# Attention and rational MLP in one kernel: keys and queries transposed by VectorE from 32 by 32 blocks, first softmax in two equal parts

## The chip, the cores and the metric

One core of one Trainium2 chip runs the whole kernel. The metric is the device time of that core in microseconds (us). The engines are called as the profile calls them: PE is TensorE's matmul, PEld its weight load, DVE is VectorE, ACT is ScalarE, POOL is GpSimd, SP is SyncE, whose queue issues the kernel's DMAs.

## The reference

There are 8 batches of 8 heads, each with 576 tokens of 64 columns, and 32 "pack" rows `p` per head.

```python
def sm_attn(qq, kk, vv):
    s = scale * np.matmul(qq, kk.transpose(0, 1, 3, 2))
    s = s - np.max(s, axis=-1, keepdims=True)
    a = np.exp(s)
    a = a / (np.sum(a, axis=-1, keepdims=True) + 1e-09)
    return np.matmul(a, vv)
p_packed = sm_attn(p, k, v)
out = sm_attn(q, p_packed, p_packed)
...
h = x @ w_in                      # x: 4608 tokens of 512, w_in 512 x 2048
P = a[0] + a[1] * h + a[2] * h2 + a[3] * h3
Q = 1.0 + np.abs(b[0]) * np.abs(h) + np.abs(b[1]) * h2
g = P / (Q + 1e-06)
return (g @ w_out).astype(np.float32)
```

The weights of the MLP come as float64 and are converted on the chip.

## The kernel before

**A planner sets the order.** The kernel's operations are recorded by a `Planner` (line 32) and issued by its `issue` (line 212) in the order of a list schedule. A table of costs per engine, a rate for DMAs (`DMA_RATE`, line 48) and the edges between operations set their ranks. Every engine then runs its own list strictly in order, so a row that waits holds back all rows behind it on that engine. All compute instructions carry one line, L216, in the profile; they are told apart by the names of their tiles.

**The MLP.** The hidden layer is worked in units of half a batch (288 tokens) by 256 of the 2048 hidden columns; a batch has 16 units. A unit (`hidden`, line 681) multiplies with PE into two tiles `h`; ACT, DVE and POOL turn them into the rational function (tiles `Y`, `U`, `sq`, `V`, 288 or 576 columns wide), and split the result into `gh` and `gl`. Three units later PE multiplies these with `w_out` into `acc` (`acc_block`, line 758). The leftover 64 tokens of a batch are gathered over two batches in `G` and multiplied in `remainder` (line 730).

**The attention of the next batch** (`attention`, line 476) is a generator whose pieces are laid between the units of the batch before. The first batch's attention stands ahead of all units, and the second's falls into the stretch in which the weights are still converted. One batch's attention goes so:

1. Keys come in two tiles of four heads, `k0` and `k1` (`load`, line 428), into a ring `nat` of two buffers that keys, values and queries share. A tile holds the first 512 tokens, 4 successive tokens of a head per partition. The 64 leftover tokens of keys and queries go into a tile `rkq`, those of the values into `rv`.
2. `transposed` (line 497) turns a tile with 8 PE transposes of 128 by 128 into PSUM, in two PSUM banks, and ACT copies each bank (128x512) into the big tile `KX` (`kx` in the profile). Four more PE transposes and a copy bring the leftover keys (`krem`).
3. Scores of the pack rows against the keys; softmax in two parts, of 256 and 320 keys. Each part keeps its own maximum. Afterwards small DVE operations and an ACT exponential (lines 548 to 554) work out factors `F` that bring the parts together.
4. PE transposes the exponentials, multiplies them with the values (one product for each part), and DVE adds the parts with `tensor_scalar` and `scalar_tensor_tensor` (lines 598 to 603). When the product has read the values, the two query loads may start (lines 593 to 595).
5. Queries are transposed as the keys were, 16 PE transposes and 4 copies, plus 4 and 2 for the leftover tokens. The next batch's keys and leftovers are loaded as buffers come free.
6. Second scores, DVE's 32 by 32 transposes of them out of PSUM, softmax, DVE transposes back, and the split into `AH` and `AL`, which the next batch's units read.

`KX` exists once, so the next batch's keys can't be put there before this batch's `AH` and `AL` are done.

Of the kernel before, what the change touches and what calls it, by code (L numbers as in the profile page):

```python
# [18 lines left out]
AF = mybir.ActivationFunctionType  # L19
# [12 lines left out]
class Planner:  # L32
# [59 lines left out]
    def transfer(self, args):  # L92
        size = mybir.dt.size(args[1].dtype)
        run = 1
        for step, n in reversed(args[1].ap):
            if step != run:
                break
            run *= n
        n = 1
        for _, m in args[1].ap:  # L100
            n *= m
        return n * size / self.DMA_RATE[run * size >= 1024]

    def price(self, engine, calls):
        if engine != "tensor":
# [83 lines left out]
    def order(self):  # L189
        n = len(self.ops)  # L190
        self.costs = [self.price(*x) for x in self.ops]
        self.transfers = [self.transfer(calls[0][1]) if engine == "sync" else 0 for engine, calls in self.ops]
        before = self.edges()
        after = [[] for _ in range(n)]
        for i, x in enumerate(before):
            for j in x:
                after[j].append(i)
        sync = [x[0] == "sync" for x in self.ops]
        rank = list(range(n))
        best = None  # L200
# [7 lines left out]
        self.t0 = best[1]; self.deps = dict(enumerate(before))  # L208
        self.end = best[0]
        return sorted(range(n), key=lambda i: (best[1][i], i))  # L210

    def issue(self):
# [35 lines left out]
def attention_rational_ffn(  # L248
# [48 lines left out]

    full_ring = Ring(sb, "full", 1, [P, DM])
    neg = full_ring.next([P, P], F32R)
    nat_ring = Ring(sb, "nat", 2, [P, 4 * NS * D])  # L300
    pn_ring = Ring(sb, "pn", 1, [P, NG, 2, D])
    rkq_ring = Ring(sb, "rkq", 1, [P, H, D])

    rv_ring = Ring(sb, "rv", 1, [P, H // 2, D])

# [117 lines left out]

    NAT, AH, AL, PPT = {}, {}, {}, {}

    def load(bb, what):
        if bb >= B:
            return  # L430
        if what == "rem":

            r, rv, pn = NAT[bb, "r"], NAT[bb, "rv"], NAT[bb, "p"] = rkq_ring.next(), rv_ring.next(), pn_ring.next()
            nc.sync.dma_start(r[0:REM], k[bb, :, NS * P : T, :].rearrange("h p d -> p h d"))
# [4 lines left out]
            for i in range(2):  # L439
                src = q[bb, 4 * i : 4 * i + 4, NS * P : T, :].rearrange("h (p x) d -> p h (x d)", x=2)  # L440
                r2 = r[REM + HREM * i : REM + HREM * (i + 1)].rearrange("p (h x) d -> p h (x d)", x=2)
                nc.sync.dma_start(r2, src)
            for i in range(2):
                src = v[bb, 4 * i : 4 * i + 4, NS * P : T, :].rearrange("h p d -> p h d")
                nc.sync.dma_start(rv[REM * i : REM * (i + 1)], src)
            return
        x, g = what[0], int(what[1])
        src = {"k": k, "q": q, "v": v}[x][bb, 4 * g : 4 * g + 4, 0 : NS * P, :]
        if bb == 0 and x != "k":
            if g == 0:  # L450
                NAT[x] = w_ring.at(NCH - 2 + "vq".index(x), [P, 2, 4 * NS * D], F32)
            t = NAT[x][:, g, :]
        else:
            t = nat_ring.next()
# [21 lines left out]
    def attention(bb):  # L476
# [30 lines left out]
        for g in range(2):  # L507
# [1 line left out]
            if bb > 0:  # L509
                load(bb, f"v{g}")  # L510
            yield
        rkq = NAT[bb, "r"]
        t = bank(bb)
        for j in range(NJ):
            nc.tensor.transpose(t[:, j * P : (j + 1) * P], rkq[:, 2 * j : 2 * j + 2, :], ident)
        nc.scalar.copy(krem, t.rearrange("p (j c) -> p j c", j=NJ)[:, :, 0:REM])
        t = bank(bb)
        for r in range(NG):
            nc.tensor.transpose(t[:, r * P : (r + 1) * P], NAT[bb, "p"][:, r, :, :], ident)
        nc.scalar.copy(pT, t[:, 0 : NG * P].rearrange("p (r c) -> p r c", r=NG))  # L520
        yield


        KEYS = ((0, 2 * P), (2 * P, T))
        of = lambda a, r: a.rearrange("p (x r) -> p x r", r=NG)[:, :, r]
        for r in range(NG):
            t = [bank(bb)[:, 0 : c1 - c0] for c0, c1 in KEYS]
            tiles(
                (
                    (t[x][cols(j), 0 : 2 * P], pT[rows(i), r, cols(j)], kmain[rows(i), r, j, :]),  # L530
                    dict(start=True, stop=True),
                )
                for j in range(NJ)
                for x, i in ((0, 1 - r), (1, r))
            )
# [12 lines left out]
        nc.vector.tensor_tensor(nbm, nb[:, 0:2], nb[:, 2:4], ALU.min)  # L548
        nc.vector.tensor_sub(xr(f), two(nbm), xr(nb))
        nc.scalar.activation(f, f, AF.Exp)  # L550
        nc.vector.tensor_mul(fs, f, sm)
        nc.vector.scalar_tensor_tensor(tot, fs[:, 0:2], 1e-9, fs[:, 2:4], ALU.add, ALU.add)
        nc.vector.reciprocal(rec, tot)
        nc.vector.tensor_mul(xr(F), xr(f), two(rec))
        yield

        for r in range(NG):
            t = bank(bb)
            for s in range(NS):
                nc.tensor.transpose(t[:, s * P : (s + 1) * P], KX[:, r, s * P : (s + 1) * P], ident)  # L560
            nc.scalar.copy(KX[:, 2 + r, 0 : NS * P], t)
            if r == 1:

                t = bank(bb)
                for i in range(NG):
                    o = slice(i * P, (i + 1) * P)
                    nc.tensor.transpose(t[:, o], KX[:, i, T - P : T], ident)
                    nc.tensor.transpose(t[0:REM, o], KX[:, i, NS * P : T], ident)
                nc.scalar.copy(eTr, t[:, 0 : NG * P])
# [1 line left out]

        t = bank(bb)
        rv = NAT[bb, "rv"]
        for r in range(NG):
# [22 lines left out]
        twice = lambda o: o.rearrange("p (i d) -> p i d", i=1).broadcast_to([P, 2, D])  # L597
        for r in range(NG):
            o = pp[:, r]
            nc.vector.tensor_scalar(o, twice(t[:, 2 * r * D : (2 * r + 1) * D]), F[:, r : r + 1], None, ALU.mult)  # L600
            nc.vector.scalar_tensor_tensor(
                o, twice(t[:, (2 * r + 1) * D : (2 * r + 2) * D]), F[:, 2 + r : 3 + r], o, ALU.mult, ALU.add
            )
            nc.tensor.transpose(t[:, (2 + r) * P : (3 + r) * P], pT[:, r, :], ident)
        nc.scalar.copy(PPT[bb], t[:, 2 * P :].rearrange("p (r c) -> p r c", r=NG))
        yield
        for g in range(2):
            transposed("q", g)
            load(bb + 1, f"k{g}")
            if g == 0:  # L610
                t = bank(bb)
                for j in range(NJ):
                    nc.tensor.transpose(t[:, j * P : (j + 1) * P], rkq[:, 2 * j : 2 * j + 2, :], ident)
                src = t.rearrange("p (i r y a c) -> p r y a i c", r=NG, y=2, a=2, i=2)[:, :, 1]
                for r in range(NG):
                    nc.scalar.copy(qx[:, r, :, HMAIN:HALF].rearrange("p (a i) c -> p a i c", a=2), src[:, r])
                load(bb + 1, "rem")
            yield

# [138 lines left out]
    def acc_block(u, i):  # L758
# [10 lines left out]
        if i == 0:  # L769
            O[bb, x] = o_ring.next()  # L770
        o = O[bb, x]
        ov = out[bb * T : bb * T + NS * P, :].rearrange("(p i x) m -> p x i m", i=2, x=2)[:, x]
        if u == NU - 1 and i == 1:
            nc.vector.tensor_copy(o[:, i, :], acc)
        else:
# [94 lines left out]
```

## Time and profile before

| | |
|---|---|
| median of 3 runs | 822.48 us (822.13 to 823.46) |
| the profiled execution | 823.16 us |
| its span, first to last instruction | 821.4 us |
| mean granted TensorE clock | 0.969 |
| stretch from 204 to 763 us: clock, PE busy | 1.00, 555.6 of 559 us |
| the DMA queue's share of the 16 engines' time | 20.9% |

Until about 140 us the weights are loaded and converted, from about 160 us to 763 us the kernel is in a steady state, and the last 58 us hold the last units. In the fences below a row of the groups names the line, the engine, the operation, `out<-in`, the shapes and the count, then busy us and mean ns of one, then the idle time of the engine before it with what ended it. A row of a timeline or of the chain has the start, the length, the engine and what it ran. A row of the stretches names the stretch and its length, then busy us and instructions of each engine, the granted clock, the mean share of the DMA engines and GB/s.

### The profile page before, as it was taken

How to read it: one execution, taken by the hardware profiler on the slowest of the kernel's cores; microseconds unless marked ns; L12 is line 12 of the kernel's file. 1: busy time of each engine (PE TensorE's matmuls, PEld its weight loads, DVE VectorE, ACT ScalarE, POOL GpSimd, SP SyncE). 2: the span in 40 equal slices, each digit the busy share in tenths (PEclk: the TensorE clock that was granted, in tenths of full speed). 3: DMA queues.
4: the chain of work that ended last, by engine and by line, in shares of the span. 5: the costliest groups of instructions: out<-in, count | busy, mean ns of one | idle time of the engine just before them, and what ended most of it. 6: DMA issues, size and time to landing. Idle time of an engine off the chain costs nothing.

```text
span 821.4 us, 15529 instructions
## 1 busy us (share of the span) xinstructions
PE 774.1 (94%) x5584; PEld 613.7 (75%) x5584; DVE 693.6 (84%) x1296; ACT 691.5 (84%) x1566; POOL 460.9 (56%) x462
## 2 busy tenths in 40 slices
PE   5677788999999999999999999999999999999997
PEld 3355565888877877788877877788877878778886
DVE  2999999888898788988798778988798788998873
ACT  5898888899797879999888869999888889898872
POOL 0006455755487546755577445755578445856663
PEclk9678798999999999999999999999999999999999
DMA  8973241010400212010400203010400210000001
GB/s 250 387 253 105 104 123 27 26 57 26 123 27 1 81 50 87 27 52 31 123 26 1 81 20 117 27 52 30 123 27 1 77 37 31 26 1 27 26 2 39
DMA packets 50941, 56.06 MB, mean 68 GB/s; under 512 B 13488, under 2 KB 40112, under 8 KB 50864
## 3 DMA queue, kind: packets, MB, share of 16 engines
q1 hardware_dynamic: 50864, 55.07, 20.9%
q8 instruction: 44, 0.72, 0.4%
q14 instruction: 33, 0.27, 0.1%
HBM read 45.62 MB, written 9.44 MB: 67 GB/s over the span
## 4 chain that ended last, share of the span: by engine, by line
PE 75%; DVE 12%; ACT 7%; DMA 2%; issue 1%; SPq 1%; POOL 0%; DVEq 0%; ACTq 0%; POOLq 0%
PE acc L216 36%; PE h L216 23%; PE at L216 16%; DVE Y L216 5%; DVE small L216 3%; DMA m<-in_moe_w_in_dram 2%; DVE w L216 2%; ACT w L216 1%; ACT V L216 1%; ACT m L216 1%; DVE V L216 1%; ACT Y L216 1%; SPq L216 1%; ACT U L216 1%; ACT kx L216 1%
## 5 line engine op out<-in xcount | busy, mean ns | idle before, releaser
L216 PE MATMUL acc<-w,gh 128*128 128x512 f32 x1024 | 330.6, 401 | 4.4 <-ACT w L216 4.4
L216 PEld LDWEIGHTS acc<-w,gh 128*128 128x128 f32 x1024 | 186.6, 190 | 47.8 <-issue 5.8
L216 POOL TENSOR_TENSOR U<-U,sq 128x576 f32<-128x576 f32 x118 | 168.8, 1431 | 73.1 <-ACT U L216 31.6
L216 POOL TENSOR_TENSOR gl<-Y,gh 128x512 fp32r<-128x512 f32 x128 | 166.2, 1299 | 65.0 <-ACT gh L216 32.2
L216 PE MATMUL acc<-w,gl 128*128 128x512 f32 x512 | 198.4, 401 | 0.0
L216 PE MATMUL h<-AH,m 128*128 128x288 f32 x1024 | 193.6, 308 | 4.5 <-DVE Y L216 4.0
L216 PEld LDWEIGHTS h<-AH,m 128*128 128x128 f32 x1024 | 160.0, 192 | 36.2 <-DVE Y L216 16.9
L216 ACT ACTIVATE Y<-h,abS 128x288 f32<-128x288 f32 x256 | 128.2, 513 | 27.6 <-PE h L216 23.8
L216 DVE TENSOR_TENSOR Y<-Y,h 128x288 f32<-128x288 f32 x256 | 111.3, 447 | 40.0 <-ACT sq L216 20.0
L216 DVE SCALAR_TENSOR_TENSOR Y<-Y,abS,V 128x576 f32<-128x576 f32 x128 | 103.4, 808 | 39.3 <-ACT V L216 38.6
L216 DVE SCALAR_TENSOR_TENSOR Y<-Y,abS,h 128x288 f32<-128x288 f32 x256 | 126.4, 507 | 3.3
L216 ACT ACTIVATE sq<-h 128x288 f32<-128x288 f32 x236 | 98.3, 422 | 33.9 <-PE h L216 31.9
L216 PEld LDWEIGHTS acc<-w,gl 128*128 128x128 f32 x512 | 96.7, 190 | 28.4 <-issue 7.7
L216 PE MATMUL h<-AL,m 128*128 128x288 f32 x512 | 112.7, 300 | 0.0
L216 POOL COPY G<-Y 128x64 f32<-128x64 f32 x128 | 34.6, 270 | 135.9 <-DVE Y L216 102.9
L216 ACT ACTIVATE U<-h 128x288 f32<-128x288 f32 x256 | 100.9, 426 | 8.5 <-DVE V L216 6.6
L216 ACT ACTIVATE V<-U,one 128x576 f32<-128x576 f32 x128 | 99.0, 774 | 8.1 <-DVE Y L216 6.5
L216 DVE SCALAR_TENSOR_TENSOR Y<-V,Y 128x576 f32<-128x576 f32 x128 | 96.1, 751 | 2.0
L216 DVE SCALAR_TENSOR_TENSOR V<-U,V 128x576 f32<-128x576 f32 x128 | 96.2, 751 | 0.0
L216 ACT CAST gh<-Y 128x512 fp32r<-128x512 f32 x128 | 82.0, 641 | 5.2 <-DVE Y L216 3.5
L216 ACT ACTIVATE V<-V 128x576 f32<-128x576 f32 x128 | 85.4, 667 | 0.4
L216 PEld LDWEIGHTS h<-AL,m 128*128 128x128 f32 x512 | 84.1, 192 | 0.3
(123 smaller groups left out, 908.3 us busy)
## 6 DMA issues: line engine op xcount, KB each, us to landing
nat<-in_k_dram SPq DMA_DIRECT2D x16, 512.0 KB, 4.0
out_dram<-o SPq DMA_DIRECT2D x15, 512.0 KB, 3.1
w<-in_moe_w_out_dram SPq DMA_DIRECT2D x14, 512.0 KB, 4.4
nat<-in_v_dram SPq DMA_DIRECT2D x14, 512.0 KB, 3.9
nat<-in_q_dram SPq DMA_DIRECT2D x14, 512.0 KB, 5.0
m<-in_moe_w_in_dram SPq DMA_DIRECT2D x8, 512.0 KB, 9.5
w<-in_moe_w_in_dram SPq DMA_DIRECT2D x8, 512.0 KB, 11.0
rkq<-in_k_dram SPq DMA_DIRECT2D x8, 128.0 KB, 4.2
```

The costliest lines, as they stand in the source:

```text
L216: getattr(getattr(self.nc, engine), name)(*args, **kwargs)
```

## The change

Nothing changes for the first batch but the place of its `rkq` tile. For the other seven:

- **Loads.** A key or query tile now has all 576 tokens of four heads. It comes in four DMAs, for even and odd tokens (`i`) and for the two halves of 32 columns (`y`). Each writes 32 partitions: token `2 t + i` of a run of 64 lies in partition `64 i + 32 y + t`, as 36 pieces of 32 columns, 128 bytes each. Before, a tile was one DMA whose pieces were 1 KB. The tile `rkq` and its loads are gone. Values come in two DMAs per tile with pieces of 512 bytes, in another order of tokens. `rv` comes in four DMAs.
- **Transposes.** DVE transposes the 32 by 32 blocks, straight from the loaded tile into `KX`: two instructions of 128x576 per tile. PE's transposes of keys and queries and ACT's copies of them are gone, as are those of `rkq`.
- **First softmax.** Two equal parts of 288 keys with one common maximum (one `tensor_scalar` per row group takes the larger and scales it), so that the factors `F`, the extra exponential and the second half of the sum of parts fall away; the two products with the values become one. The matmuls of the scores are cut into 256 and 32 columns, since the second part begins in the middle of the tokens' order.
- **Planner and output.** `DMA_RATE` gets a third value, 100, for pieces under 256 bytes. Rows of the output go to other places in the same tile, in pieces of the same size.

```diff
-    DMA_RATE = 190.0, 370.0
+    DMA_RATE = 100.0, 190.0, 370.0
...
+            src = src.rearrange("h t d -> (h t) d")
+            for i in range(2):
+                for y in range(2):
+                    o = 64 * i + 32 * y
+                    blocks = src[:, 32 * y : 32 * y + 32].rearrange("(a t i) d -> i t a d", t=32, i=2)[i]
+                    nc.sync.dma_start(t[o : o + 32].rearrange("p (a d) -> p a d", d=32), blocks)
+            return
...
         def transposed(x, g):
-            for r in range(NG):
+            for r in range(NG if bb > 0 else 0):
+
+                src = NAT[bb, f"{x}{g}"].rearrange("p (j r c) -> p r j c", j=2, r=NG)[:, r]
+                nc.vector.transpose(qx[:, r, 2 * g : 2 * g + 2, :], src)
+            for r in range(NG if bb == 0 else 0):
                 t = bank(bb)
...
-        KEYS = ((0, 2 * P), (2 * P, T))
+        KEYS = ((0, 2 * P), (2 * P, T)) if bb == 0 else ((0, HALF), (HALF, T))
...
+                for x in range(2):
+                    nc.vector.reduce_max(mx[:, 2 * x + r : 2 * x + r + 1], t[x], axis=AX.X)
+                bias = nbm[:, r : r + 1]
+                nc.vector.tensor_scalar(bias, mx[:, r : r + 1], mx[:, 2 + r : 3 + r], -SCALE, ALU.max, ALU.mult)
+                for x, (c0, c1) in enumerate(KEYS):
+                    i = slice(2 * x + r, 2 * x + r + 1)
+                    nc.scalar.activation(KX[:, r, c0:c1], t[x], AF.Exp, bias=bias, scale=SCALE, accum_out=sm[:, i])
...
-        nc.vector.tensor_tensor(nbm, nb[:, 0:2], nb[:, 2:4], ALU.min)
-        nc.vector.tensor_sub(xr(f), two(nbm), xr(nb))
-        nc.scalar.activation(f, f, AF.Exp)
-        nc.vector.tensor_mul(fs, f, sm)
+        if bb == 0:
...
+        else:
+            fs = sm
         nc.vector.scalar_tensor_tensor(tot, fs[:, 0:2], 1e-9, fs[:, 2:4], ALU.add, ALU.add)
         nc.vector.reciprocal(rec, tot)
-        nc.vector.tensor_mul(xr(F), xr(f), two(rec))
+        if bb == 0:
+            nc.vector.tensor_mul(xr(F), xr(f), two(rec))
...
+            if bb > 0:
+                nc.vector.tensor_scalar(o, twice(t[:, r * D : (r + 1) * D]), rec[:, r : r + 1], None, ALU.mult)
+            else:
...
-            if g == 0:
+            if g == 0 and bb == 0:
                 t = bank(bb)
                 for j in range(NJ):
                     nc.tensor.transpose(t[:, j * P : (j + 1) * P], rkq[:, 2 * j : 2 * j + 2, :], ident)
```

**The order on DVE at the fifth batch's queries.** First the list before, from DVE's work on the units around the query transposes up to the second scores' transposes. `Y_56`, `V_56` and `h_113` are tiles of the units, `kx_5` is the fifth batch's `KX`, and `at_144` is a PSUM bank with its second scores.

```order
L216 SCALAR_TENSOR_TENSOR Y_56_791<-Y_56_791,abS,V_56_790 128x576
L216 SCALAR_TENSOR_TENSOR V_56_790<-U_56_789,V_56_790 128x2x288
L216 TENSOR_TENSOR Y_57_806<-Y_57_806,h_114_809 128x288
L216 SCALAR_TENSOR_TENSOR Y_56_791<-V_56_790,Y_56_791 128x576
L216 SCALAR_TENSOR_TENSOR Y_57_806<-Y_57_806,abS,h_114_809 128x288
L216 TENSOR_TENSOR Y_58_817<-Y_58_817,h_115_819 128x288
L216 SCALAR_TENSOR_TENSOR Y_58_817<-Y_58_817,abS,h_115_819 128x288
L216 STREAM_TRANSPOSE kx_5_718<-at_144_820 128x288
L216 STREAM_TRANSPOSE kx_5_718<-at_145_821 128x288
```

The same place now; `nat_25` and `nat_26` are the two query tiles, and `at_104` is the bank with the scores.

```order
L216 STREAM_TRANSPOSE kx_5_684<-nat_25_748 128x576
L216 SCALAR_TENSOR_TENSOR Y_58_763<-Y_58_763,abS,h_113_765 128x288
L216 STREAM_TRANSPOSE kx_5_684<-nat_25_748 128x576
L216 SCALAR_TENSOR_TENSOR Y_57_752<-Y_57_752,abS,V_56_751 128x576
L216 TENSOR_TENSOR Y_58_763<-Y_58_763,h_114_766 128x288
L216 SCALAR_TENSOR_TENSOR V_56_751<-U_56_750,V_56_751 128x2x288
L216 SCALAR_TENSOR_TENSOR Y_58_763<-Y_58_763,abS,h_114_766 128x288
L216 SCALAR_TENSOR_TENSOR Y_57_752<-V_56_751,Y_57_752 128x576
L216 TENSOR_TENSOR Y_59_772<-Y_59_772,h_115_774 128x288
L216 STREAM_TRANSPOSE kx_5_684<-nat_26_749 128x576
L216 SCALAR_TENSOR_TENSOR Y_59_772<-Y_59_772,abS,h_115_774 128x288
L216 STREAM_TRANSPOSE kx_5_684<-nat_26_749 128x576
```

Four instructions of 128x576 now stand between the units' work, and each waits in DVE's own list for a query DMA, with the units' rows behind it.

**The order on SP at the same place.** Before, from the query loads to the store of a finished half batch (`o_13`):

```order
L216 DMA nat_25_787<-in_q_dram 128x4x256
L216 DMA nat_26_788<-in_q_dram 128x4x256
L216 DMA rv_6_802<-in_v_dram 64x4x64 x2
L216 DMA nat_27_799<-in_k_dram 128x4x256
L216 DMA rkq_6_801<-in_k_dram 64x8x64
L216 DMA rkq_6_801<-in_q_dram 32x4x128 x2
L216 DMA nat_28_814<-in_k_dram 128x4x256
L216 DMA out_dram<-o_13_830 256x1x512
```

And now:

```order
L216 DMA nat_25_748<-in_q_dram 32x36x32 x4
L216 DMA nat_26_749<-in_q_dram 32x36x32 x4
L216 DMA rv_6_759<-in_v_dram 32x4x64 x4
L216 DMA nat_27_758<-in_k_dram 32x36x32 x4
L216 DMA nat_28_769<-in_k_dram 32x36x32 x4
L216 DMA out_dram<-o_13_785 128x2x512
```

Nine loads have become twenty, in the same turn; the store still stands behind them all.

More of the change, by code (lines that the diff above doesn't have):

```diff
@@ L453, in load @@
         else:
-            t = nat_ring.next()
+            t = nat_ring.next()[:, 0 : 4 * NS * D]
         t = t.rearrange("p (h s d) -> p h s d", h=4, s=NS)
@@ L511, in attention @@
             yield
[L512 to L516, printed above, removed]
+        rkq = NAT.get((bb, "r"))
+        if bb == 0:
+            t = bank(bb)
+            for j in range(NJ):
+                nc.tensor.transpose(t[:, j * P : (j + 1) * P], rkq[:, 2 * j : 2 * j + 2, :], ident)
+            nc.scalar.copy(krem, t.rearrange("p (j c) -> p j c", j=NJ)[:, :, 0:REM])
         t = bank(bb)
@@ L527, in attention @@
             t = [bank(bb)[:, 0 : c1 - c0] for c0, c1 in KEYS]
+            if bb > 0:
+                for b in (slice(0, 2 * P), slice(2 * P, HALF)):
+                    tiles(
+                        (
+                            (t[x][cols(j), o], pT[rows(x), r, cols(j)], qx[rows(x), r, j, b]),
+                            dict(start=True, stop=True),
+                        )
+                        for j in range(NJ)
+                        for x, o in ((0, b), (1, slice((b.start + HREM) % HALF, (b.stop + HREM - 1) % HALF + 1)))
+                    )
+                for x in range(2):
[5 more added lines that the diff above has]
+                    nc.scalar.activation(KX[:, r, c0:c1], t[x], AF.Exp, bias=bias, scale=SCALE, accum_out=sm[:, i])
+                if r == 0:
+                    yield
+                continue
             tiles(
@@ L559, in attention @@
             for s in range(NS):
-                nc.tensor.transpose(t[:, s * P : (s + 1) * P], KX[:, r, s * P : (s + 1) * P], ident)
+                c0 = s * P + (REM if bb > 0 and s > 1 else 0)
+                nc.tensor.transpose(t[:, s * P : (s + 1) * P], KX[:, r, c0 : c0 + P], ident)
             nc.scalar.copy(KX[:, 2 + r, 0 : NS * P], t)
@@ L573, in attention @@
         rv = NAT[bb, "rv"]
-        for r in range(NG):
+        for r in range(NG if bb > 0 else 0):
+            tiles(
+                (
+                    (
+                        t[cols(j), r * D : (r + 1) * D],
+                        KX[:, 2 + r, s * P + 32 * j : s * P + 32 * j + 32]
+                        if s < NS
+                        else eTr[rows(j // 2), r * P + 32 * j : r * P + 32 * j + 32],
+                        NAT[bb, f"v{j // 2}"][:, 2 * (j % 2) + r, 2 * (s % 2) + s // 2, :]
+                        if s < NS
+                        else rv[rows(j // 2), 2 * (j % 2) + r, :],
+                    ),
+                    dict(start=s == 0, stop=s == NS),
+                )
+                for s in range(NS + 1)
+                for j in range(NJ)
+            )
+        for r in range(NG if bb == 0 else 0):
             for x, blocks in enumerate((range(2), range(2, NS + 1))):
```

57 lines of the change are left out of this document (41 added, 16 removed).

## Prediction

> **What bounds the kernel now.** I read the page's busy shares first, then stretches of the span, then the waits and the chain in the steady state.
>
> ```profile
> PE 774.1 (94%) x5584; PEld 613.7 (75%) x5584; DVE 693.6 (84%) x1296; ACT 691.5 (84%) x1566; POOL 460.9 (56%) x462
> ```
>
> No engine is idle enough to be ignored, and 84% is an average over stages. The stretches, with busy us of PE, PEld, DVE, ACT and POOL in this order, part them:
>
> ```profile
> 40.00:140.00 100.00, 79.11 (x567) 56.45 (x560) 97.04 (x163) 88.62 (x180) 43.29 (x37) 0.84 0.41 130
> 204.00:763.00 559.00, 555.62 (x4083) 447.13 (x4076) 479.87 (x910) 481.25 (x1120) 344.83 (x345) 1.00 0.16 48
> ```
>
> There are two regimes. From 40 to 140 us, where the weights are converted and the second batch's attention runs, DVE is busy 97.04 of 100 us and PE 79: DVE is the bound. From 204 to 763 us, six batches of about 93 us, PE is busy 99% at clock 1.00, DVE and ACT 86%. The waits in that stretch (engine, waited for, us, times, longest):
>
> ```profile
> DVE Y L216 <- ACT V L216: 29.7, 45, 1.9
> DVE Y L216 <- ACT sq L216: 17.3, 19, 1.8
> DVE Y L216 <- ACT U L216: 11.8, 29, 1.3
> ...
> PE h L216 <- DVE Y L216: 2.4, 8, 0.8
> ```
>
> DVE idles 79 us of the 559, and 58.8 us of that waits for ACT. PE hardly waits. But the chain of waits is not PE alone; here is a piece of it behind one batch's second scores:
>
> ```profile
> 406.88 0.78 PE at L216 x16
> 407.66 0.83 DVE kx L216 x2
> 408.49 1.49 DVE Y L216 x3
> 409.98 0.67 DVE V L216
> 410.65 0.52 DVE small L216
> ...
> 425.05 1.24 DVE Y L216 x3
> ...
> 426.34 1.86 PE h L216 x12
> ```
>
> It comes back to PE at 426 us. So DVE sets the pace for some 18 us around the second softmax, and the same place in each batch is where the change adds DVE work. Two such stretches, from the query transposes to where the new order has the next batch's key transposes:
>
> ```profile
> 297.00:355.20 58.20, 57.60 (x454) 45.66 (x453) 53.60 (x104) 51.44 (x121) 36.64 (x36) 1.00 0.20 62
> 390.20:448.50 58.30, 57.54 (x431) 46.59 (x430) 50.91 (x95) 49.16 (x111) 40.17 (x40) 1.00 0.17 53
> ```
>
> DVE is at 92% and 87% there, PE at 99%.
>
> **PE's transposes go.** A busy mean of overlapping matmuls overstates them, so I take the distance between starts in the timeline of PE:
>
> ```profile
> 397.18 1.04 PE L216 MATMUL at<-ident,nat 128*128 128x128 f32 x8
> 397.97 0.78 PE L216 MATMUL h<-AH,m 128*128 128x288 f32 x4
> ...
> 398.86 0.60 PE L216 MATMUL at<-ident,rkq 128*128 128x128 f32 x4
> 399.21 0.71 PE L216 MATMUL acc<-w,gh 128*128 128x512 f32 x2
> ```
>
> Eight take 0.79 us and four of `rkq` 0.35 us. A batch loses 32 and 8 of them: 4 x 0.79 + 2 x 0.35 = 3.9 us of PE. Where PE is the bound, over six batches, that is 23.2 us at most. In the 40 to 140 us stretch, where the seventh of them lies, it is nothing, since PE has 21 us free.
>
> **DVE's transposes come, ACT's copies go.** The rows for it (DVE first, then ACT; the first row is DVE's transpose of the same size in the second softmax):
>
> ```profile
> L216 DVE STREAM_TRANSPOSE kx<-kx 128x576 f32<-128x576 f32 x16 | 12.2, 762 | 0.0
> L216 DVE TENSOR_TENSOR small<-small 128x4 f32<-128x4 f32 x24 | 7.3, 303 | 1.4 <-ACT small L216 1.2
> L216 DVE TENSOR_TENSOR small<-small 128x2 f32<-128x2 f32 x8 | 1.2, 151 | 0.1
> L216 DVE SCALAR_TENSOR_TENSOR small<-at,small 128x128 f32<-128x128 f32 x14 | 4.8, 344 | 0.1
> ...
> L216 ACT COPY kx<-at 128x512 f32<-128x512 f32 x74 | 43.3, 613 | 6.1 <-PE at L216 6.0
> L216 ACT COPY kx<-at 128x128 f32<-128x128 f32 x16 | 4.0, 289 | 0.6 <-PE at L216 0.6
> L216 ACT COPY kx<-at 128x256 f32<-128x256 f32 x8 | 3.2, 396 | 1.4 <-PE at L216 1.3
> L216 ACT ACTIVATE small<-small 128x4 f32<-128x4 f32 x8 | 1.8, 226 | 0.3 <-DVE small L216 0.3
> ```
>
> DVE gains 8 x 0.762 = 6.1 us a batch. It loses three operations of 0.303, one of 0.151 and two sums of 0.344 us, together 1.75 us: net +4.35 us. ACT loses 8 x 0.613 + 2 x 0.289 + 0.396 + 0.226 = 6.1 us. ACT is no bound, but its shorter list cuts into the 58.8 us that DVE waits for it.
>
> *What this does in the steady state.* On average DVE goes from 80.0 to 84.3 us a batch and PE's span from 93.2 to 89.3, so DVE would be at 94%. The best that the trace shows over a long stretch is 97.04 of 100. If the planner spreads the new work evenly, the whole 23.2 us come out. Taken stretch by stretch it looks otherwise. In the two stretches above DVE gets 6.1 us and loses the 0.7 us of the sums: 53.6 + 5.4 = 59.0 and 50.9 + 5.4 = 56.3 us. At 97% these need 60.8 and 58.0 us, against 58.2 and 58.3 now: +1.15 us a batch in the mean, +7 us over six. The truth lies between -23.2 and +7. The places in the order say that the new transposes sit inside the dense stretches (none is moved to the loose middle of the batch), but units can shift around them and ACT gives way. I have no row that says how much, and take the middle: -8.1 us.
>
> A rule of the Trainium skill speaks for the exchange: "VectorE: DVE Perf Modes", section "The three transpose paths", gives 390 ns on TensorE and 311 ns on VectorE for a 128 by 128 square in bf16. This trace has 99 ns for PE and, for a block of 576 columns, 762 ns or 169 ns for each 128 columns of DVE, so its order does not hold here. By the page's two figures (an estimate) a batch would take 12.5 us from PE and give 11.2 us to DVE, a worse bargain for DVE than the sum above has.
>
> *In the 40 to 140 us stretch* the +4.35 us fall on an engine with 2.96 us free. Between +1.4 us (all idle time filled) and +4.35; the nearest row is its own 97%, so I take +4.3 us.
>
> **Loads.** What a piece costs is read from the DMA share of two lone groups of transfers: four `pn` loads (64 pieces of 256 bytes each) and two value tiles (512 pieces of 1 KB each). Columns: stretch, length, PE, clock, DMA share, GB/s.
>
> ```profile
> 187.00:191.00 4.00, 4.00 (x44) 1.00 0.08 16
> 454.00:458.00 4.00, 4.00 (x20) 1.00 0.39 131
> ```
>
> 4 x 0.08 x 16 engines / 256 = 20 ns for 256 bytes; in the second stretch, which holds one value tile, 4 x 0.39 x 16 / 512 = 49 ns for 1 KB. For 128 bytes the line through both gives 15 ns, and more than 49 ns is excluded by the larger piece; the nearest row is 20 ns. A tile has 4 x 576 x 2 = 4608 pieces: 5.8 us (4.3 to 14.1), where 512 KB now take 1.6. The loads and their users, in the timelines of SP and PE:
>
> ```profile
> 392.34 0.94 SPq L216 DMA_DIRECT2D nat<-in_q_dram  x2
> ...
> 406.81 0.47 PE L216 MATMUL at<-kx,ppT 64*32 64x288 f32 x8
> ```
>
> ```profile
> 398.25 0.37 SPq L216 DMA_DIRECT2D nat<-in_k_dram  x1
> ...
> 452.90 0.60 PE L216 MATMUL at<-ident,nat 128*128 128x128 f32 x4
> ```
>
> ```profile
> 454.10 5.94 SPq L216 DMA_DIRECT2D nat<-in_v_dram  x2
> ...
> 488.65 0.65 PE L216 MATMUL at<-nat,kx 128*32 128x64 f32 x32
> ...
> nat<-in_q_dram SPq DMA_DIRECT2D x14, 512.0 KB, 5.0
> ```
>
> Keys have 55 us and values 34. Queries have less.
>
> From the issue of the query loads to the second scores it is 14.5 us. With two tiles at 5.8 us, 2 us from issue to the first bytes (5.0 us median to landing in the last row, less two tiles of 1.6) and the last two transposes, 1.5 us, it is 15.1 us: about as now. So I cost the loads at nothing in the steady state; the cover is those 14.5 us. At the start the second batch's two key tiles stand ahead of weights on SP and add 2 x 4.2 = 8.4 us of transfers. DVE's longest wait for a DMA is this one:
>
> ```profile
> DVE abS L216 <- DMA ab<-in_moe_a_dram: 1.4, 1, 1.4
> ```
>
> So DVE's other work covers the weights' transfers now: nothing, 8.4 us if that cover is gone. The store of `o_13` behind twenty loads waits for the key buffers as before: nothing.
>
> **Small things.** The scores have the same columns in more matmuls: nothing, at most another 0.7 us of PE a batch, by the narrow ones of now (16 of the 120 records a batch):
>
> ```profile
> L216 PE MATMUL at<-kx,small 64*32 64x64 f32 x120 | 5.0, 232 | 0.0
> ```
>
> The two products with the values have the same matmuls. One output row order for another, pieces of the same size: nothing. The first softmax's chain is four DVE operations shorter, which helps the queries' loads start earlier; no gain is counted.
>
> **The sum.** -8.1 in the steady state, +4.3 at the start, -3.8 us in all. The profiled execution has 823.16 us, the median is 822.48, 0.7 lower; on the median's scale 818.7 us. With 2 us unsure at the start, and 4 to 5 in the steady state, this case runs from 812 to 825.
>
> **Rivals.**
>
> *DVE takes over as the bound.* Slower. Place: from the query transposes to the next key transposes, 58 of each 93 us. Price: +7 in the steady state and +4.3 at the start, 834 us. It decides where DVE's list in that stretch is longer than PE's, 59.0 against 57.6 - 3.9 us. For it: the chain lies on DVE there already, and the transposes were PE work that other PE work overlapped, while DVE runs one thing at a time. Against it: 58.8 of DVE's 79 us of idle time are ACT's doing, and ACT's list gets shorter.
>
> *The full relief.* The planner spreads the work, DVE reaches 94%: -23.2 + 4.3, 803.6 us. For it: DVE does 97% early. Against it: there PE was the one to wait, and here both must be nearly full at once.
>
> *Late queries.* Slower. If a piece of 128 bytes costs more than the 256-byte rows say, the query transposes stand at the head of DVE's list with the units' rows behind them. At 30 ns a tile takes 8.6 us, the scores come 6.3 us later, and seven batches lose 44 us: 863 us. From 20 ns up it begins. Against it: 256 bytes at 20 ns. The Trainium skill warns of this: "DMA: Bandwidth & Descriptors", section "Specifications", asks for at least 512 bytes for line rate and names a read-modify-write below; the `pn` rows show cheaper pieces at 256 bytes and no such penalty, and no row here shows 128.
>
> **Numbers.** What a measurement of this kernel can tell from no change is about 0.2%, 1.65 us, so faster is under 820.8 and slower over 824.1 us. My forecast has 0.46 (faster 0.32, same 0.10, slower 0.04); DVE as the bound 0.29 (same 0.04, slower 0.25); full relief 0.18, all faster; late queries 0.07, all slower. That makes 0.50, 0.14 and 0.36. The signs are divided, and the likeliest case's own range is 812 to 825. The range of 803 to 834 us takes in the first three cases and leaves out late queries and the outer ends.
>
> **What would show it.** Right: no `at<-ident,nat` for the later batches on PE, `STREAM_TRANSPOSE kx<-nat` at about 0.76 us x56, batches of about 92 us in the steady state with DVE near 92% and PE still above 97%, and DVE waits for ACT well under 58.8 us. DVE as the bound: PE below 97% in the stretches behind the queries, with PE's `h` waiting for `Y`. Full relief: batches of 89 us. Late queries: DVE `kx` waiting for DMA `nat<-in_q_dram`, microseconds at a time. Wrong at the start: the first 204 us longer by much other than 4 us. A DVE transpose from `nat` well off 0.76 us would make the whole sum wrong.

## The result and the profile after

| | before | changed |
|---|---|---|
| median | 822.76 us (822.13 to 823.46, 4 runs) | 809.36 us (808.45 to 809.83, 4 runs) |
| the profiled execution | 823.16 us | 808.45 us |
| its span | 821.4 us | 806.7 us |

The ratio is 0.983, with a 95% interval of 0.981 to 0.985: 1.7% or 13.4 us faster. The forecast of 818.7 us had the sign, but only 3.8 of the 14.7 us by which the profiled execution became shorter. Busy times on the page of the changed kernel:

```profile
PE 745.5 (92%) x5416; PEld 585.4 (73%) x5416; DVE 709.1 (88%) x1310; ACT 666.0 (83%) x1482; POOL 463.9 (58%) x462
```

PE lost 28.6 us and ACT 25.5, DVE gained 15.5. To see where the time came out I cut both spans at one event, the issue of the third batch's query loads on SP (205.3 us before, 209.3 now). Behind it lie six batches in the steady state and the end. The stretches of the kernel before (from, to, length, then busy us of PE, PEld, DVE, ACT and POOL, the clock, the DMA share, GB/s):

```profile
0.00:205.30 205.30, 166.26 (x1310) 122.47 (x1314) 176.40 (x324) 174.16 (x366) 85.43 (x86) 0.88 0.41 136
205.30:821.40 616.10, 607.85 (x4278) 491.20 (x4278) 517.24 (x974) 517.34 (x1201) 375.49 (x377) 1.00 0.15 46
```

The same two of the changed kernel, and its 40 to 140 us, which the prediction spoke of:

```profile
0.00:209.30 209.30, 159.20 (x1277) 116.35 (x1281) 181.55 (x328) 167.37 (x347) 87.98 (x86) 0.84 0.50 133
209.30:806.70 597.40, 586.35 (x4143) 469.07 (x4143) 527.57 (x983) 498.67 (x1136) 375.90 (x377) 1.00 0.25 47
...
40.00:140.00 100.00, 73.21 (x504) 52.64 (x504) 93.59 (x148) 82.75 (x159) 42.79 (x35) 0.76 0.56 141
```

The start became 4.0 us longer and the rest 18.7 us shorter. In the rest PE lost 21.5 us of work, its idle time (length less busy) went from 8.2 to 11.1 us, and that is the 18.7. DVE's busy time grew by 10.3 us. The cut leaves the third batch's keys in the start, so the rest holds 22 of the 28 tiles of new transposes and five of the seven first softmaxes, five and a half batches' worth; by the sum's own prices that is 24.1 us for DVE (44 x 0.762 - 5 x 1.06 - 12 x 0.344) and 21.2 us off PE (22 x 0.79 + 11 x 0.35). The new transposes themselves are as forecast, and nothing is waited for ahead of them (last column 0.0):

```profile
L216 DVE STREAM_TRANSPOSE kx<-nat 128x576 f32<-128x576 f32 x56 | 42.7, 768 | 0.0
...
L216 DVE TENSOR_SCALAR small<-small 128x18 f32<-128x18 f32 x16 | 5.8, 366 | 0.0
...
L216 DVE TENSOR_SCALAR small<-small 128x1 f32<-128x1 f32 x14 | 3.0, 211 | 0.0
```

The waits of five batches, from the third to the eighth batch's query loads, 469.2 us before and 453.1 now, or 93.8 and 90.6 a batch (engine, waited for, us, times, longest). Rows of the kernel before for the same five batches:

```profile
DVE Y L216 <- ACT V L216: 25.4, 34, 1.9
DVE Y L216 <- ACT sq L216: 15.5, 16, 1.8
DVE Y L216 <- ACT U L216: 10.5, 22, 1.3
...
DVE Y L216 <- ACT Y L216: 1.1, 3, 0.5
```

And of the changed one:

```profile
DVE Y L216 <- ACT V L216: 12.3, 27, 1.5
...
DVE Y L216 <- ACT Y L216: 10.1, 9, 3.4
...
DVE Y L216 <- ACT U L216: 3.2, 9, 0.6
...
PE acc L216 <- ACT gh L216: 2.9, 7, 0.7
...
DVE Y L216 <- ACT sq L216: 2.8, 7, 0.8
...
PE h L216 <- DVE Y L216: 0.8, 2, 0.4
```

DVE's time for the transposes came out of its waits for ACT, 52.5 us in these four rows before and 28.4 now. PE hardly waits for DVE. The stretch that the prediction feared, from the query transposes to the next key transposes, is this in the fourth and the sixth batch, first before:

```profile
304.00:360.00 56.00, 56.00 (x378) 44.98 (x379) 50.80 (x97) 50.23 (x116) 36.91 (x37) 1.00 0.25 74
490.70:546.00 55.30, 55.30 (x379) 44.90 (x378) 49.30 (x95) 49.66 (x113) 36.11 (x37) 1.00 0.24 75
```

And now, with all eight new transposes of a batch in each:

```profile
305.20:361.00 55.80, 54.79 (x394) 41.42 (x392) 53.69 (x104) 47.59 (x106) 36.70 (x37) 1.00 0.42 74
483.80:539.00 55.20, 54.19 (x386) 40.83 (x387) 53.08 (x104) 47.04 (x104) 36.22 (x37) 1.00 0.44 68
```

DVE is busy 96% of them where it was busy 91% and 89%, and PE 98% where it was 100%. Behind the fifth batch's query transposes, the changed kernel's chain of waits is a piece of PE alone up to the second scores:

```profile
397.92 0.80 PE h L216 x6
398.72 0.93 PE acc L216 x4
399.64 0.80 PE h L216 x6
400.44 1.84 PE acc L216 x8
402.28 0.80 PE h L216 x6
403.08 0.93 PE acc L216 x4
404.01 0.65 PE at L216 x16
```

Behind those scores, where DVE had the chain for some 18 us, ACT has it from 409.8 to 416.1 us and then PE again.

### The profile page after: what moved, and what is told of

Its sections match the earlier page's. It is cut to its first block, busy times and chain, and to the rows that moved or that the text cites. A ratio compares the mean times of both kernels' runs of the same rounds, so it can differ in the third digit from the quotient of the medians.

```text
span 806.7 us, 15198 instructions
## 1 busy us (share of the span) xinstructions
PE 745.5 (92%) x5416; PEld 585.4 (73%) x5416; DVE 709.1 (88%) x1310; ACT 666.0 (83%) x1482; POOL 463.9 (58%) x462
## 3 DMA queue, kind: packets, MB, share of 16 engines
q1 hardware_dynamic: 168800, 55.07, 31.4%
## 4 chain that ended last, share of the span: by engine, by line
PE 70%; DVE 10%; ACT 8%; SPq 4%; DMA 4%; issue 2%; POOL 1%; DVEq 0%; POOLq 0%
PE acc L216 35%; PE h L216 22%; PE at L216 13%; DVE Y L216 5%; SPq L216 4%; ACT Y L216 2%; DVE w L216 1%; ACT U L216 1%; ACT V L216 1%; ACT w L216 1%; DMA w<-in_q_dram 1%; ACT sq L216 1%; DVE V L216 1%; POOL w L216 1%; DVE kx L216 1%
## 5 line engine op out<-in xcount | busy, mean ns | idle before, releaser
L216 PE MATMUL acc<-w,gl 128*128 128x512 f32 x512 | 193.2, 398 | 0.3 <-POOL gl L216 0.3
L216 PEld LDWEIGHTS h<-AH,m 128*128 128x128 f32 x1024 | 162.7, 195 | 40.5 <-DVE Y L216 23.1
L216 ACT ACTIVATE Y<-h,abS 128x288 f32<-128x288 f32 x256 | 125.2, 509 | 23.5 <-PE h L216 19.3
L216 ACT ACTIVATE U<-h 128x288 f32<-128x288 f32 x256 | 98.1, 421 | 8.7 <-PE h L216 4.3
```

The source lines that it names most:

```text
L216: getattr(getattr(self.nc, engine), name)(*args, **kwargs)
```

## The experiments

Theory 1: PE sets the pace of the steady state, its removed transposes are the gain. Rival 2: it is ACT's removed copies, since DVE waited for ACT. Rival 3: it is the shorter softmax. Rival 4: DVE is at its limit in the dense stretches, and what it is given shows. For the start: the amount of DVE work, the key loads ahead of the weights, or the planned order. Twelve kernels ran. "Start" is the time to the third batch's query loads in the profiled run, "rest" what follows, with PE's and DVE's busy time in the rest. A ratio is to runs of the kernel before on the same chip, whose medians lay between 822.8 and 824.1 us. Start and rest come from one profiled run each, and the cut can lie a few PE instructions earlier or later in the units' work, so differences of 2 us in them are not told apart.

| kernel | median us | ratio to before, 95% | start | rest | PE | DVE |
|---|---|---|---|---|---|---|
| before | 822.76 | | 205.3 | 616.1 | 607.9 | 517.2 |
| changed | 809.36 | 0.983 (0.981 to 0.985) | 209.3 | 597.4 | 586.4 | 527.6 |
| e1 softmax alone | 827.45 | 1.004 (1.002 to 1.006) | 212.2 | 614.5 | 605.0 | 505.5 |
| e2 transposes alone | 811.18 | 0.984 (0.981 to 0.987) | 212.3 | 598.0 | 585.7 | 535.8 |
| e3 PE's transposes back | 830.32 | 1.007 (1.005 to 1.010) | 214.7 | 614.3 | 606.7 | 531.8 |
| e4 PE's and ACT's back | 828.94 | 1.006 (1.003 to 1.008) | 214.5 | 613.7 | 607.5 | 531.1 |
| e5 ACT's back | 807.85 | 0.981 (0.977 to 0.985) | 208.0 | 598.3 | 587.8 | 530.0 |
| e6 DVE's twice | 832.79 | 1.011 (1.007 to 1.015) | 212.6 | 618.7 | 598.6 | 556.8 |
| e7 big pieces | 801.90 | 0.973 (0.969 to 0.978) | 208.4 | 590.5 | 581.5 | 526.3 |
| e8 second batch as before | 803.74 | 0.976 (0.973 to 0.980) | 204.6 | 597.3 | 586.5 | 528.2 |
| e9 softmax from the third batch | 822.87 | 0.999 (0.998 to 1.001) | 206.2 | 614.8 | 605.2 | 505.8 |
| e10 before, three rounds | 823.74 | 1.000 (0.999 to 1.001) | 204.8 | 616.9 | 608.4 | 514.8 |
| e11 old DMA rate | 807.65 | 0.980 (0.978 to 0.983) | 211.0 | 594.5 | 584.0 | 527.9 |
| e12 DVE's half twice | 825.16 | 1.002 (1.000 to 1.003) | 211.2 | 609.2 | 592.4 | 543.7 |

**e1, the softmax alone**, on the kernel before, with the parts still of 256 and 320 keys:

```diff
+            if bb > 0:
+                nc.vector.tensor_scalar(bias, mx[:, r : r + 1], mx[:, 2 + r : 3 + r], -SCALE, ALU.max, ALU.mult)
...
+        if bb == 0:
+            nc.vector.tensor_tensor(nbm, nb[:, 0:2], nb[:, 2:4], ALU.min)
...
+        else:
+            fs = sm
```

> The kernel before with the new first softmax alone: one common maximum for the two parts (still 256 and 320 keys), no factors, one product with the values; keys and queries still go through PE and ACT. Theory 1 (the gain is PE's removed transposes, nearly whole, and PE stays the bound): PE loses nothing here, so 821 to 823.5 us, no change. Rival 3 (the gain is the softmax's shorter chain and DVE's lighter list): 810 to 814 us.

DVE's work in the rest fell by 11.7 us and the time there by 1.6: DVE's relief is worth little while PE has 605 us to do. The start was 6.9 us longer, with no transposes and no new loads, which puts the time above both expected ranges. Rival 3 falls.

**e2, the transposes alone**: the changed kernel with the old operations of the softmax put back, with factors of one.

```diff
+                nc.vector.tensor_scalar(of(nb, r), of(mx, r), -SCALE, None, ALU.mult)
...
+            nc.vector.tensor_tensor(tot, nb[:, 0:2], nb[:, 2:4], ALU.min)
+            nc.vector.tensor_sub(xr(f), two(nbm), two(tot))
+            nc.scalar.activation(f, f, AF.Exp)
+            nc.vector.tensor_mul(fs, f, sm)
...
```

> The changed kernel with the old first softmax's operations put back on DVE and ACT (a second scaling of maxima, the smaller of two, difference, exponential, two products, a second pass over the product with the values, all with factors that come out as 1 or add 0). Theory 1: PE's relief is all there, DVE's list is 2 to 3 us a batch longer and has room, so 809 to 813 us. Rival 3: 818 us or more.

The rest is 598.0 us, 0.6 more than in the changed kernel, though DVE has 8.2 us more to do in it. All of the gain is in the exchange of the transposes.

**e3, PE's transposes back**: 128x128 transposes into PSUM banks that nobody reads, as many as before, beside everything of the changed kernel.

```diff
                 nc.vector.transpose(qx[:, r, 2 * g : 2 * g + 2, :], src)
+                t = bank(bb)
+                for o in range(4):
+                    tile = NAT[bb, f"{x}{g}"][:, (4 * r + o) * P : (4 * r + o + 1) * P]
+                    nc.tensor.transpose(t[:, o * P : (o + 1) * P], tile, ident)
...
```

> The changed kernel with as many PE transposes as were removed (32 of the loaded tiles and 8 of the values' leftovers a batch) put back, their results read by nobody; no ACT copies. Theory 1: PE is the bound, so six batches in the steady state get 3.9 us each and the total comes to 826 to 833 us, above the kernel before since the start keeps its 4 us. Rival (DVE or ACT bounds the changed kernel and PE has room): 810 to 815 us.

The rest, in the stretches of this kernel:

```profile
214.70:829.00 614.30, 606.70 (x4359) 493.36 (x4359) 531.76 (x984) 495.85 (x1136) 374.97 (x377) 1.00 0.25 46
```

PE is busy 606.7 of 614.3 us. The removed transposes that the rest holds, 21.2 us, brought PE 20.4 us of busy time and the rest 16.9 us. PE's idle time fell from 11.1 to 7.6 us, so no new waits came with them, for instance for the PSUM banks that they take. With 5.4 us at the start it is 22.3 us, and 21 in the median. That is theory 1.

**e4 and e5, ACT's copies back**, with PE's (e4) and without (e5). In e5, ahead of nothing that needs them:

```diff
...
                 nc.vector.transpose(qx[:, r, 2 * g : 2 * g + 2, :], src)
+                nc.scalar.copy(spare, NAT[bb, f"{x}{g}"][:, 512 * r : 512 * r + 512])
```

> As the run with PE's transposes put back, and with ACT's copies of their banks too (8 of 128x512, one of 256 and two of 128 columns a batch, into a spare tile that nobody reads). Theory 1: within 3 us of that run, since ACT is no bound. Rival 2 (what let DVE take the transposes is ACT's shorter list, 6.1 us a batch): 8 us or more above that run.

> The changed kernel with eight ACT copies of 128x512 a batch put back (from the loaded key and query tiles into a spare tile that nobody reads), PE untouched. Theory 1 (PE stays the bound and ACT is none): 809 to 813 us. Rival 2 (ACT's relief carried the gain): 818 to 833 us.

e4 is 1.4 us below e3, and e5 1.5 us below the changed kernel (and 1.2 below its expected range), though ACT has 24 and 19 us more to do in the rest. Rival 2 falls. In the changed kernel's waits of the five batches ACT itself waits for PE most, which fits:

```profile
ACT sq L216 <- PE h L216: 20.5, 45, 1.4
```

**e6 and e12, DVE's transposes twice**, all of them and every second one:

```diff
-                nc.vector.transpose(qx[:, r, 2 * g : 2 * g + 2, :], src)
+                for _ in range(2):
+                    nc.vector.transpose(qx[:, r, 2 * g : 2 * g + 2, :], src)
```

> The changed kernel with each new DVE transpose done twice, 6.1 us more of DVE a batch. Theory 1 with room on DVE: its busy time goes from 81.9 to 88 us of a 90.6 us batch, so the room is nearly used up and part of the work shows: 813 to 825 us. Rival 4 (DVE is the bound of the changed kernel already): all of it shows, 43 us in seven batches, 845 to 853 us.

> The changed kernel with every second of DVE's new transposes done twice: 3.05 us more of DVE a batch, half of what the run with all doubled had (that one: 832.8 us, 17.8 us of 30.5 in five batches showed). If DVE has room for about 2.5 us a batch and everything beyond shows, five batches take 453 to 457 us and the whole 809 to 815 us. If DVE is the bound already in the dense stretches and a fixed share of what is added shows (58%), five batches take 462 us and the whole 820 us.

The rest in e12, and then in e6:

```profile
211.20:820.40 609.20, 592.35 (x4147) 468.24 (x4146) 543.74 (x1008) 499.48 (x1138) 376.73 (x377) 1.00 0.26 46
```

```profile
212.60:831.30 618.70, 598.57 (x4172) 474.48 (x4172) 556.79 (x1038) 502.60 (x1148) 379.86 (x381) 1.00 0.25 46
```

Half of the doubling (22 transposes of 0.76 us in the rest, 16.8 us) cost 11.8 us there, the whole of it (33.5 us) 21.3: 70% and 64%. Over the five batches it was 65% and 58%. The first half cost at least as much as the second, so the room of 2.5 us a batch, which I had read out of e6, isn't there: e12 was to take 809 to 815 us by it, and took 825.2, five more than the rival. e6 itself fell between its two expected ranges.

Rival 4 is right for the stretch behind the query loads. In the fourth batch DVE was busy 53.69 of 55.8 us there in the changed kernel, 53.41 of 55.8 in e12 (307.6 to 363.4 us) and 54.81 of 57.5 in e6 (314.8 to 372.3). That is 95 to 96% in all three, while PE fell from 98% to 92% and 93%: DVE gets no further there, and work added to it takes PE's time. It isn't right for the whole rest. There PE is idle 11.1 us in the changed kernel, here 16.9 and 20.1, and DVE gets to 88%, 89% and 90%. The place counts and not only the amount: of e2's 8.2 us of added DVE work 0.5 lie in that stretch (54.15 of 55.8 us), and they cost 0.6 us in all.

Two cautions. Of e12's 11.8 us, 6.0 are in PE's busy time, with four instructions more than in the changed kernel, so PE's busy time isn't fixed by its work alone. And the profiled run of e12 was the fastest of its twelve (822.17 to 827.05 us), so its cost is rather more than 11.8 us.

**e7, big pieces**: the key and query tiles come in pieces of 1 KB and 512 bytes, the same bytes in other places, so that what is computed from them is not the attention.

```diff
...
+            main = src[:, 0 : NS * P, :].rearrange("h (p s) d -> p h s d", s=NS)
+            nc.sync.dma_start(t[:, 0 : 4 * NS * D].rearrange("p (h s d) -> p h s d", h=4, s=NS), main)
+            rest = src[:, NS * P : T, :].rearrange("h (p s) d -> h p (s d)", s=2)
+            for h in range(4):
+                nc.sync.dma_start(t[32 * h : 32 * h + 32, 4 * NS * D :], rest[h])
```

> The changed kernel with key and query tiles of all but the first batch loaded in pieces of 1 KB and 512 bytes, the same bytes in the wrong places, so the output is another; no DMA of 128-byte pieces is left. If the later start (third batch's query loads at 209.3 us instead of 205.3) comes from the second batch's key loads standing ahead of weights, the start returns to about 205 us and the total is 803 to 806 us. If it comes from DVE's additional work in the second batch, nothing changes: 808 to 810 us. If queries are late in the steady state, below 803 us.

It took 801.9 us, 7.5 less than the changed kernel, nearly all of it in the rest (6.9, with nine PE instructions fewer behind the cut). So either the small pieces or the order that goes with them were not free. The queries' path, in the changed kernel, on SP, DVE and PE:

```profile
387.13 7.63 SPq L216 DMA_DIRECT2D nat<-in_q_dram  x8
```

```profile
397.15 0.77 DVE L216 STREAM_TRANSPOSE kx<-nat 128x576 f32<-128x576 f32 x1
...
403.46 0.77 DVE L216 STREAM_TRANSPOSE kx<-nat 128x576 f32<-128x576 f32 x1
```

```profile
403.94 0.71 PE L216 MATMUL at<-kx,ppT 64*32 64x288 f32 x16
```

From issue to the scores it is 16.8 us; in e7 the loads were issued at 386.71 and the scores began at 396.47, 9.8 us.

**e11, the planner's old rate for small pieces**, everything else as changed:

```diff
-    DMA_RATE = 100.0, 190.0, 370.0
+    DMA_RATE = 190.0, 190.0, 370.0
```

> The changed kernel with the planner's rate for small pieces back at the value of before (190 in place of 100): the same instructions, in another order. If the planner must know that the small pieces are slow, the queries' transposes are planned too early and DVE's list waits for them: some 0.5 us for each of 28 tiles, 815 to 820 us, with DVE waiting for the query tiles' DMAs in the trace. If the loads have room in any plan, 807 to 812 us. Theory B on the start adds up to 5 us either way at the third batch's query loads (209.3 us in the changed kernel).

The planner now puts the query transposes earlier, and DVE waits for the loads, but little:

```profile
DVE kx L216 <- DMA nat<-in_q_dram: 2.1, 4, 0.7
```

At this batch the scores came 12.5 us behind the loads (388.70 to 401.21), 4.3 us sooner than in the changed kernel, and the time is 807.65 us. Over the five batches e11 took 455.4 us, the changed kernel 453.1 and e7 449.2, so the earlier place alone didn't shorten them; that e11's rest is 2.9 us shorter comes from its end, 139.1 us against 144.3. e7's gain is not explained by this order. But e7 has other prices in the planner and so an order of its own, and whether its gain comes from the loads themselves (SP's time, the traffic, a later landing) or from that order isn't shown.

**e8, the second batch as before**, the other six in the new way:

```diff
-        if bb > 0:
+        if bb > OLD:
             t = NAT[bb, what] = nat_ring.next()
...
-            for r in range(NG if bb > 0 else 0):
+            for r in range(NG if bb > OLD else 0):
...
-        KEYS = ((0, 2 * P), (2 * P, T)) if bb == 0 else ((0, HALF), (HALF, T))
+        KEYS = ((0, 2 * P), (2 * P, T)) if bb <= OLD else ((0, HALF), (HALF, T))
```

> The changed kernel with the second batch too in the old way (loads of 1 KB pieces, PE transposes, ACT copies, softmax in two unequal parts); batches three to eight as changed. Its attention falls into the conversion of the weights, where PE had room. Both explanations of the start, DVE's work and the loads, expect the 4 us back: 804 to 807 us, below both kernels. If the start's 4 us are only the order that the planner happened on: 808 to 811 us.

The start is back at 204.6 us and the rest stays at 597.3: 803.74 us, better than both kernels. Of all here only e7, whose data lie in other places, is faster.

**e9, the new softmax from the third batch on**, on the kernel before, and **e10, the kernel before in another order**:

```diff
-            if bb > 0:
+            if bb > 1:
                 nc.vector.tensor_scalar(bias, mx[:, r : r + 1], mx[:, 2 + r : 3 + r], -SCALE, ALU.max, ALU.mult)
```

```diff
-    ROUNDS = 4
+    ROUNDS = 3
```

> The kernel before with the new first softmax for the third to eighth batch only; the second batch's attention is computed as before. The softmax for the second batch too gave 827.4 us, with the third batch's query loads at 212.2 us where the kernel before has 205.3. Theory A (the new softmax in the second batch itself costs the start): query loads of the third batch at 205 to 207 us, and 820 to 823 us in all. Theory B (any new list of operations gives another plan for the weights' stretch, and the start moves with the plan, not with what the second batch does): the start stays at 209 to 214 us and the time at 824 to 829 us. The steady state is expected as in the kernel before in both, 469 us over five batches.

> The kernel before with the planner's rounds cut from four to three: the same instructions, in another order. It tells how much the time of these operations depends on the planned order alone. Theory B (the start moves with the plan): the third batch's query loads move by 2 us or more from 205.3, in either direction, and the whole by 2 to 8 us. Theory A (the start is set by the amount of work): within 1 us at the start, within 2 us in all.

In e9 the start is 206.2 us, in e10 204.8. The four kernels whose second batch is computed in the old way have 204.6 to 206.2 us, the ten others 208.0 to 214.7. A new order for the same work moved the start by 0.5 us and the median by nothing that can be told (in e11, by 1.7 us). So it goes with the second batch's new way that the start is longer, and theory B, in which any plan does it, falls in this form.

## Why the prediction was wrong in its size

**The bound.** It named PE as the bound of the steady state, and ACT's busy share as of no account. e3, e4 and e5 show both.

**PE's transposes.** The price was right: the rest holds 21.2 us of them by the rows, and its PE time fell by 21.5. The sum's 23.2 us counted six batches where its stretch has five and a half, since the third batch's keys come before 204 us.

**The failed step** is the weighing behind it: "I have no row that says how much, and take the middle: -8.1 us". The steady state gave -18.7. The upper end, +7, came from DVE's list in the dense stretches, 59.0 and 56.3 us, where the old list was kept and 5.4 us were laid on top. The runs show DVE busy 53.7 and 53.1 us in such stretches with all eight transposes in them, 2.9 and 3.8 more than before, and PE at 98%. The ceiling of 97% was not the fault, for DVE reaches 96% there; the length of the list was. Two things made it shorter.

First, DVE got less net work than summed: +10.3 us in the rest where the sum's prices give 24.1. The groups' rows account for it. The 128x18 `tensor_scalar` took 3.6 us less than before, the scaling of the maxima 2.6 less (ten of 128x2 went, ten of 128x1 came), the units' own rows 3.4 less, the removed operations of 128x4 columns 1.5 more than priced, and a 128x2 sum 1.3 more than before. The last 4.3 us are records that overlap: the groups' times add up to 564.9 us before and 579.6 now, against 517.2 and 527.6 us of busy time.

Second, the order did shift around the transposes, as the full relief wanted: DVE's waits for ACT fell by 24 us in five batches, and PE was idle only 2.8 us more in the whole rest.

**Full relief** had 0.18 and 803.6 us, and was nearest to what happened: 18.7 of the 21.2 us came out, and a batch took 90.6 us, where full relief says 89 and the forecast 92. But DVE didn't reach its 94%. It is busy 409.5 of 453.1 us in the five batches, 90%, because of the work that it didn't get.

**DVE as the bound** had 0.29. Its sign, PE below 97% behind the queries and `h` waiting for `Y`, isn't there: PE is at 98% in those stretches and waits 0.8 us in five batches. But e12 shows how near it was: with 3.05 us more a batch PE is at 92% there and all the gain is gone.

**Loads at nothing** is not settled. With big pieces 7.5 us more came out, and how much of that belongs to the loads isn't shown. The price of a piece was about right: in two stretches that hold two query tiles together (9216 pieces, and some 80 KB of other loads)

```profile
388.50:392.90 4.40, 4.40 (x24) 3.70 (x23) 3.84 (x8) 3.88 (x10) 2.94 (x3) 1.00 0.83 122
392.90:398.20 5.30, 5.30 (x32) 4.73 (x31) 4.58 (x9) 4.51 (x12) 3.10 (x4) 1.00 1.11 137
```

the DMA share makes (4.40 x 0.83 + 5.30 x 1.11) x 16 / 9216 = 16.5 ns at most, between the 15 of the line and the 20 that I took. These stretches carry 122 and 137 GB/s at shares of 0.83 and 1.11, 147 and 123 at a full share; the value tile that the prediction quoted had 131 at 0.39, 336 at a full share. The Trainium skill's rule on this ("DMA: Bandwidth & Descriptors", section "Specifications": at least 512 bytes for line rate) is borne out in that; no row shows the read-modify-write that it names. The late queries as I priced them, 44 us, didn't come: the scores began 16.8 us behind the loads and not 14.5, but PE had units to do meanwhile, as the chain above shows. e11 says the same: 4.3 us sooner at that place, and the five batches didn't get shorter.

**The start** was +4.0 us where I had +4.3, which was luck, for the reason doesn't hold. I had DVE fill its last idle time from 40 to 140 us, yet there it is busy 93.6 us where it was 97.0, and e1 loses 6.9 us with fewer instructions on DVE. Nor is it the key loads alone: e7 gets back 0.9 us. e8 and e9 show that it goes with the second batch's new way. How is open. A wait of PE for the conversion of the weights, before and then in the changed kernel, and POOL's last step for the weights in the changed kernel and then before:

```profile
PE acc L216 <- ACT w L216: 4.4, 1, 4.4
```

```profile
PE acc L216 <- ACT w L216: 15.0, 4, 4.9
```

```profile
147.57 1.31 POOL L216 TENSOR_TENSOR w<-o,w 128x512 fp32r<-128x512 f32 x1
```

```profile
140.84 1.30 POOL L216 TENSOR_TENSOR w<-o,w 128x512 fp32r<-128x512 f32 x1 [2.59 <-ACT w L216]
```

PE waits for ACT's conversions of the weights, which end later. In e9 this step starts at 140.9 us and in e1 at 147.6, but in e8, with the best start of all, at 144.1. Nor does the wait sort the starts: up to 215 us it is 2.7 us in e3, whose start is the longest, and 15.4 in e5, whose start is the shortest of the ten. The granted clock does: from 40 to 140 us its mean is 0.84 to 0.87 in the four kernels with the old second batch and 0.73 to 0.82 in the ten others. Whether that is a cause, or only follows from PE's having less to do, isn't shown. A run that keeps the second batch's new work and fixes only the order of the conversions wasn't made.

## What to carry to other kernels

Where one engine is busy 99% for hundreds of microseconds, work taken off it can come out nearly whole (here 18.7 of 21.2 us), as long as the receiver's added time fits into waits that it already has. Read the receiver's waits, and do not lay new work on top of its busy time in one stretch as though nothing else in it would move. How near the receiver is to its limit is told by doubling half of the added work in the same place: here 65 to 70% of it showed, while other work of the same engine at another place was nearly free. And where a stage has another bound, try the change without that stage: leaving the second batch as it was gave 5.6 us more.

## What the runs showed of the hardware that was not expected

- `tensor_scalar` on DVE with two columns took 491 ns in the mean where one with a second operand and one column took 211, and the same 128x18 instruction 589 ns before and 366 after; the size of the data says little at this scale, and no run shows why.
- A 32 by 32 block transpose of 128x576 takes 768 ns in its record, and added 0.66 to 0.74 us to DVE's busy time where it stood among others (29.2 us for 44 in e6, 16.2 us for 22 in e12).
- Loads in pieces of 128 bytes raised the queue's share of the DMA engines' time from 20.9% to 31.4% of the span for the same 55 MB, and with big pieces it was 21.4%.
